# One fused attention and expert kernel on one core: other first steps, a plain product for the row of maxima, and new orders of the pairs

## The chip, the cores and the metric

The kernel runs on one core of a Trainium2 chip. The metric is the device time of one execution in microseconds (us); the program is built for that core alone and uses no other. Engines are named as the profile names them: PE (TensorE, matrix products; PEld are its weight loads), DVE (VectorE), ACT (ScalarE), POOL (GpSimd) and SP (SyncE, which here only issues DMAs).

## The reference

All inputs are float32. Attention with pooled queries comes first, then a soft mixture of experts, then a gated network:

```python
q_pool = q.reshape(B, H, S // 2, 2, D).mean(axis=3)            # B, H, S, D = 4, 8, 1152, 64
scores = q_pool @ k.transpose(0, 1, 3, 2) / np.sqrt(D)
attn = np.exp(scores - scores.max(-1, keepdims=True))
attn = attn / (attn.sum(-1, keepdims=True) + 1e-9)
x = (attn @ v).transpose(0, 2, 1, 3).reshape(2304, 512)
logits = x @ phi                                               # 8 experts x 4 slots
d = softmax of logits over the tokens; slot_input = d.T @ x
slot_out[e] = relu(slot_input[e] @ w1[e]) @ w2[e]
x = softmax of logits over the slots @ slot_out
xn = x / sqrt(mean(x * x) + 1e-6) * rms_g
out = (silu(xn @ w_gate) * (xn @ w_val)) @ w_out
```

The change touches attention alone, the first 430 us or so.

## The kernel before, in words

**Pairs.** The 32 heads of attention are worked on two at a time, in 16 pairs; one head of a pair lies in partitions 0 to 63, the other in 64 to 127. A pair has 576 pooled queries, cut in two halves `h` of 288, and 1152 keys, cut in nine tiles `kt` of 128.

- `qk` (a step `q31` is tile 3, half 1; lines 374 to 388): a score tile, the keys in partitions and 288 queries of each head in columns, in a double bank of PSUM. Four products of each head are added up: high keys by high queries, low keys by high queries, high keys by low queries (keys and queries are split into a rounded part and a rest), and `pick` by `mr`, which subtracts each query's maximum. ACT then writes `e`, the exponential.
- `add_e` (a step `e31`): POOL adds up `e` over the tiles, for the sums. The first of each group adds nothing.
- `av` (a step `v31`, or `v3` for both halves; lines 403 to 412): the products of `e` and the values, in plain float32, four products side by side, each with 32 columns of weights.
- `max_item` (a step `m`; lines 289 to 335): products of queries and keys whose maximum DVE reads straight from PSUM. Pair 0 has 14 of them, of 384 columns; the eight with numbers 0 to 7 run before the first score, and 0 to 2 and 3 to 5 are the queries' first two tiles with the three chunks of keys, 6 and 7 the products with `tb`, the last 64 queries of both heads in one block. The later pairs have eleven of up to 512 columns, of which `ta` and `tb` stand in the pair before.
- The nine maxima of a query tile set are reduced once more (`max_red`), turned into a row by TensorE (`max_row`, lines 342 to 347), negated by ACT into `mrow`, and copied into `mr` by four DMAs (`send_row`). In pair 0 a first part goes another way, without DMA: `first_max` turns the maxima by products with an identity, and DVE spreads the result over `mr` in one scaling (lines 359 to 371). `row_0` is `max_row` and `send_row` of pair 0's rest.

**Side steps.** While a pair p runs, its list of steps also prepares later pairs and finishes earlier ones: `load_q`, `load_k`, `sum_q`, `round_k`, `high_q`, `block_q` (which fills `tb`), `less_k` for p + 2; `rest_k`, `low_q`, `load_v`, `max_red`, `max_row`, `send_row` for p + 1; `take_x`, `sums`, `inverse`, `x_logits`, `x_turn`, `recips`, `logit_add`, `x_divide` for p - 1 (the sums are inverted, the outputs turned and divided). Every fourth pair adds a softmax over tokens (`d_turn`, `d_exp`, `d_back`, `d_copy`, `slot_part`, `slot_copy`, `slot_turn`) or over slots (`c_turn`, `c_exp`, `c_soft`). Weights of the last network come as 64-bit data by `load_64`, are converted by ACT (`abs_64`, two instructions) and DVE (`turn_64`), and are written back to memory by `spill`.

**Order.** The order is written out by hand in lists: `FIRST` for pair 0, `PLAN` for pairs 1 to 13, `LAST_2` for pair 14, `LAST` for pair 15. Each engine and each queue of DMAs (SP's, and POOL's for `rest_k` and `sum_q`) works on its own steps in the order of the list, and waits only for data or for room. PSUM's eight banks are four double banks in attention: one holds `av` from its first product to `take_x`, and score tiles, maxima and all small results share the rest. Steps that find no room in SBUF for a weight leave their load to a later step.

**The start.** Lines 790 to 837 stand ahead of the lists. SP loads pair 0's queries and keys in chunks; ACT rounds three chunks of keys, `kc`; DVE and POOL add up the queries; `block_q(0)` fills `tb`; then come the eight first maxima and `first_max`. `hold` (lines 198 to 201) issues products that nothing reads; the kernel uses it only behind attention.

Of the kernel before, what the change touches and what calls it, by code (L numbers as in the profile page):

```python
# [31 lines left out]
NMAX = 9  # L32
AHEAD = 0
FIRST = """
m m round_k1 round_k1 less_1 m rest_1 q00 q10 m e10 m m q70 m q20 q30 e30 q50 q40 load_q m row_0 q60 m e50 block_q1
q80 e20 v50 m e60 m m v30 e70 v20 e40 v60 v10 sum_q q61 q01 low_q q21 q31 q51 e31 e00 q41 m e41 q81 q11 e01 q71 m e81
m v40 e11 e71 m m max_red v70 v01 e51 e21 v00 high_q load_k block_q e61 round_k round_k e80 v80 v31 max_row load_v tb
less_k ta v21 v41 v51 send_row v11 v71 v61 v81
"""
PLAN = """  # L40
take_x load_q m load_k sum_q q00 q01 q10 m q11 q20 e00 q21 m e01 e10 e20 e11 c_exp q30 e30 q31 rest_k q40 load_ew e21
c_soft m e31 q41 e40 q50 e41 m e50 q51 q60 q61 q70 turn_64 m load_ew spill e60 q71 q80 q81 round_k round_k m m m e70
e51 load_v e80 sums v0 v1 abs_64 e61 abs_64 e71 v2 d_back load_64 e81 max_red v3 v4 x_logits less_k inverse d_copy
inverse high_q block_q c_soft max_row low_q x_turn recips abs_64 logit_add slot_part c_soft pair_up x_divide x_divide
turn_64 v5 v6 d_turn send_row tb c_turn ta slot_copy turn_64 d_exp drop_x slot_turn c_soft v7 load_64 load_64 v8
"""
LAST_2 = """
take_x load_q m load_k sum_q q00 q01 load q10 m q11 load q20 e00 load q21 m e01 e10 e20 e11 c_exp load q30 e30 q31
rest_k load q40 load_ew e21 c_soft m e31 load q41 e40 load q50 e41 m e50 q51 load q60 load q61 q70 turn_64 m load_ew
spill e60 q71 load q80 q81 round_k round_k m m m e70 e51 load_v e80 sums v0 v1 abs_64 e61 abs_64 e71 v2 d_back load_64  # L50
e81 max_red v3 v4 x_logits less_k inverse d_copy inverse high_q block_q c_soft max_row low_q x_turn recips abs_64
logit_add slot_part c_soft pair_up x_divide x_divide turn_64 v5 v6 d_turn send_row tb c_turn ta slot_copy turn_64
d_exp drop_x slot_turn c_soft v7 load_64 load_64 v8
"""
LAST = """
take_x q00 load_64 sum_up sum_up load_q load_k load q01 e00 e01 c_exp turn_64 load_ew load q10 load q11 spill e10 e11
# [39 lines left out]
def attention_softmoe_gated_kernel(ctx: ExitStack, tc: tile.TileContext, kT, qT, vv, ip, cst, w1, w2, wg, wv, wo, rg, out):  # L96
    nc = tc.nc
    dv, ac, pe, gp, sy = nc.vector, nc.scalar, nc.tensor, nc.gpsimd, nc.sync
# [18 lines left out]
    def A(shape, dt, name):  # L117
        return take("A", shape, dt, name)
# [53 lines left out]
    def S(shape, name, dt=F32, bufs=2, tag=None):  # L172
        return small.tile(shape, dt, tag=tag or name, name=name, bufs=bufs)

    def two_banks(name):
        return ps.tile([128, 2, 512], F32, tag="u", bufs=4, name=name)
# [27 lines left out]
    ident, stack = cs[:, 0:128], cs[:, 128:256]  # L204
# [9 lines left out]
    mxw = one.tile([128, 128], F32, name="mxw")  # L214
    sall = one.tile([32, 5], F32, name="sall")
    mr = [one.tile([128, 576], F32R, name=f"mr{i}") for i in range(2)]
    pick = [one.tile([128, 128], F32R, name=f"pick{i}") for i in range(2)]
    tb = one.tile([128, 128], F32R, name="tb")
# [41 lines left out]
    def block_q(p):  # L260

        for s in range(2):
            r = slice(64 * s, 64 * s + 64)
            ac.copy(tb[r, r], qh[p][r, 512:576] if p else qh[p][r, 256:320])
# [24 lines left out]
    def max_item(p, i):  # L289

        if p not in mx3:
            mx3[p] = S([128, 2 * NQT + 1, 3], "mx3")
        if p:
            return wide_item(p, i)
        o = two_banks("mxp")
        if i not in (6, 7):
            t, c = divmod(i - 2 if i > 7 else i, 3)
            at = 128 * t if t < 2 else 128 * t + 64
            for s in range(2):
                r = slice(64 * s, 64 * s + 64)  # L300
                pe.matmul(o[:, s, 0:KC], lhsT=qh[p][r, at:at + 128], rhs=kh[p][r, KC * c:KC * c + KC], start=True, stop=True)
            to = mx3[p][:, 0:2 * NQT].rearrange("p (s t) c -> p s t c", s=2)[:, :, t, c]
            dv.reduce_max(out=to, in_=o[:, :, 0:KC], axis=AX.X)
        else:
            n = 8 - i
            for j in range(n):
                c = 2 * (i - 6) + j
                pe.matmul(o[:, j, 0:KC], lhsT=tb, rhs=kh[p][:, KC * c:KC * c + KC], start=True, stop=True)
            dv.reduce_max(out=mx3[p][:, 2 * NQT, 2 * (i - 6):2 * (i - 6) + n], in_=o[:, 0:n, 0:KC], axis=AX.X)

    def wide_item(p, i):

        o = two_banks("mxp")
        q, k, m = qh[p], kh[p], mx3[p]
        heads = m[:, 0:2 * NQT].rearrange("p (s t) c -> p s t c", s=2)
        rest = slice(1024, 1152)
        if i < 8:
            c, t = divmod(i, 4)
            for s in range(2):
                r = slice(64 * s, 64 * s + 64)  # L320
                pe.matmul(o[:, s, :], lhsT=q[r, 128 * t:128 * t + 128], rhs=k[r, 512 * c:512 * c + 512], start=True, stop=True)  # L321
            dv.reduce_max(out=heads[:, :, t, c], in_=o, axis=AX.X)  # L322
        elif i == 8:
            for t in range(NQT):
                for s in range(2):
                    r = slice(64 * s, 64 * s + 64)
                    pe.matmul(o[:, s, 128 * t:128 * t + 128], lhsT=q[r, 128 * t:128 * t + 128], rhs=k[r, rest], start=True, stop=True)  # L327
            dv.reduce_max(out=heads[:, :, :, 2], in_=o.rearrange("p s (t k) -> p s t k", t=NQT), axis=AX.X)
        elif i == 9:
            for c in range(2):  # L330
                pe.matmul(o[:, c, :], lhsT=tb, rhs=k[:, 512 * c:512 * c + 512], start=True, stop=True)  # L331
            dv.reduce_max(out=m[:, 2 * NQT, 0:2], in_=o, axis=AX.X)
        else:
            pe.matmul(o[:, 0, 0:128], lhsT=tb, rhs=k[:, rest], start=True, stop=True)
            dv.reduce_max(out=m[:, 2 * NQT, 2:3], in_=o[:, 0:1, 0:128], axis=AX.X)
# [6 lines left out]
    def max_row(p):  # L342
        n = 2 * NQT + 1
        o = bank([128, 128], "mxt")
        pe.transpose(out=o[0:32], in_=mxw[:, 0:32], identity=ident)
        rows[p] = S([n, 128], "mrow", F32R, bufs=1)
        ac.mul(rows[p], o[0:n], -1.0)

# [7 lines left out]
            sy.dma_start(out=f(to[:, 0:512]).rearrange("p (t i) -> p t i", i=128), in_=f(row[NQT * s:NQT * s + NQT, :]))  # L356
            sy.dma_start(out=f(to[:, 512:576]), in_=f(row[2 * NQT:2 * NQT + 1, 64 * s:64 * s + 64]))

    def first_max():

        dv.reduce_max(out=mxa[0:64, 2:3], in_=mx3[0][0:64, 2 * NQT, 0:3], axis=AX.X)
        dv.reduce_max(out=mxb[64:128, 66:67], in_=mx3[0][64:128, 2 * NQT, 0:3], axis=AX.X)
        dv.reduce_max(out=mxa.rearrange("p (s c) -> p s c", s=2)[:, :, 0:2],
                      in_=mx3[0][:, 0:2 * NQT].rearrange("p (s t) c -> p s t c", s=2)[:, :, 0:2], axis=AX.X)
        o = bank([128, 128], "mxt")
        r = slice(0, 67)
        pe.matmul(o[r], lhsT=mxa[:, r], rhs=ident, start=True, stop=False)
        pe.matmul(o[r, 0:64], lhsT=mxb, rhs=ident[:, 64:128], start=False, stop=True)
        dv.scalar_tensor_tensor(out=mr[0][r, 0:384].rearrange("p (t i) -> p t i", t=3),
                                in0=o[r, None, :].to_broadcast([67, 3, 128]), scalar=-1.0,  # L370
                                in1=stack[r, 0:3, None].to_broadcast([67, 3, 128]), op0=ALU.mult, op1=ALU.mult)
# [249 lines left out]
    n = HELD_O  # L621
# [167 lines left out]
    with tc.manual_schedule():  # L789
        q0 = qraw[0] = A([128, 2, 576], F32, "qraw")  # L790
        k0 = kraw[0] = A([128, 1152], F32, "kraw")
        mxa = mxw
        mxb = S([128, 67], "mxb", bufs=1, tag="ct")
        qa, qb = slice(0, 384), slice(384, 576)
        kc = [slice(KC * c, KC * c + KC) for c in range(3)]
# [6 lines left out]
        kh0 = kh[0] = A([128, 1152], F32R, "kh")  # L802
# [10 lines left out]
        qs0 = qs[0] = B([128, 576], F32, "qs")  # L813
        qh0 = qh[0] = B([128, 576], F32R, "qh")
        dv.tensor_tensor(out=qh0[:, qa], in0=q0[:, 0, qa], in1=q0[:, 1, qa], op=ALU.add)
        for c in kc:
            ac.copy(kh0[:, c], k0[:, c])
        gp.tensor_tensor(out=qs0[:, qa], in0=q0[:, 0, qa], in1=q0[:, 1, qa], op=ALU.add)
        low_k(0, kc[0], gp)
        gp.tensor_tensor(out=qs0[:, qb], in0=q0[:, 0, qb], in1=q0[:, 1, qb], op=ALU.add)  # L820
        rel("A")
        ac.copy(qh0[:, qb], qs0[:, qb])
        block_q(0)
        low_q(0, gp)
        low_k(0, kc[1], gp)
        low_k(0, kc[2], gp)
# [1 line left out]
        high_q(1)  # L828
        load_v(0)
        load_k(1)  # L830
        for i in (0, 1, 2, 6, 7, 3, 4, 5):
            max_item(0, i)
        first_max()
        dv.memset(half, -0.5)
        sy.dma_start(out=ipt, in_=ip.rearrange("p (a b) -> p a b", a=4))
# [46 lines left out]
        o = accum("xl")  # L882
# [6 lines left out]
        r = rr[l]  # L889
        o = accum("by")  # L890
# [20 lines left out]
        for i in range(3):  # L911
            for s in range(2):
                c = slice(64 * s, 64 * s + 64)
# [33 lines left out]
        o = bank([128, 3, 32], "br")  # L947
# [10 lines left out]
        o = bank([128, 4, 32], "pto")  # L958
# [156 lines left out]
        o = bank([128, 4, 32], "gto")  # L1115
# [6 lines left out]
        o = bank([128, 32], "gram")  # L1122
# [118 lines left out]
        for step in SEQ:  # L1241
            n = int(step[1:] or 0)
# [29 lines left out]
        for g in range(1, NG):  # L1272
            for t in range(3):
                for c in [slice(0, 512)] if (g, t) != (NG - 1, 2) else [slice(128 * i, 128 * i + 128 * n) for i, n in TAIL]:
                    o = ps.tile([128, c.stop - c.start], F32, tag="av", bufs=2, name="yo")
# [42 lines left out]
```

## Time and profile before

| | |
|---|---|
| median of 3 runs | 680.61 us (680.22 to 681.07) |
| profiled execution | 682.14 us, its span 680.4 us |
| PE busy | 663.7 us, 98% of the span |
| DVE, ACT, POOL busy | 432.7, 403.6, 457.4 us |
| HBM traffic | 99.29 MB read, 14.16 MB written |

The span runs from the first to the last instruction of the profiled execution. A line of a timeline gives the start, the duration of all that it merges, the engine, the line of the kernel, the operation, what it writes and reads with the shapes, how many instructions (x2), and in brackets the idle time of the engine before it and what ended that. Matrix products are pipelined: each one's duration includes the time until its result is out, so that the pace is read from the starts. A line of the chain of waits gives the start, the share of time and the work that the end hung on just then.

### The profile page before, as it was taken

How to read it: one execution, taken by the hardware profiler on the slowest of the kernel's cores; microseconds unless marked ns; L12 is line 12 of the kernel's file. 1: busy time of each engine (PE TensorE's matmuls, PEld its weight loads, DVE VectorE, ACT ScalarE, POOL GpSimd, SP SyncE). 2: the span in 40 equal slices, each digit the busy share in tenths (PEclk: the TensorE clock that was granted, in tenths of full speed). 3: DMA queues.
4: the chain of work that ended last, by engine and by line, in shares of the span. 5: the costliest groups of instructions: out<-in, count | busy, mean ns of one | idle time of the engine just before them, and what ended most of it. 6: DMA issues, size and time to landing. Idle time of an engine off the chain costs nothing.

```text
span 680.4 us, 17782 instructions
## 1 busy us (share of the span) xinstructions
PE 663.7 (98%) x7319; PEld 487.2 (72%) x7319; DVE 432.7 (64%) x595; ACT 403.6 (59%) x814; POOL 457.4 (67%) x368
## 2 busy tenths in 40 slices
PE   3999999999999999999999999999899999999998
PEld 2776876866876866867767766543577788888887
DVE  5867678877888887888887766420546755444410
ACT  4566867967768868768867625331456645444420
POOL 6689789989969989789899675000357754534420
PEclk9999999999999999999999999999999999999999
DMA  6333855976966965666675659899940100000000
GB/s 224 105 121 60 242 153 157 289 233 150 265 224 183 302 189 131 185 213 164 191 204 135 228 158 341 304 347 390 385 183 1 47 32 32 15 32 32 31 32 31
DMA packets 57784, 114.66 MB, mean 169 GB/s; under 512 B 6252, under 2 KB 20072, under 8 KB 57704
## 3 DMA queue, kind: packets, MB, share of 16 engines
q1 hardware_dynamic: 53672, 100.86, 43.2%
q0 software_dynamic: 4032, 12.68, 10.7%
q8 instruction: 57, 0.93, 0.5%
q14 instruction: 23, 0.19, 0.1%
HBM read 99.29 MB, written 14.16 MB: 167 GB/s over the span
## 4 chain that ended last, share of the span: by engine, by line
PE 87%; DVE 4%; DMA 4%; issue 1%; ACT 1%; POOL 1%; DVEq 0%; POOLq 0%; ACTq 0%; SPq 0%
PE sc L383 22%; PE av L408 21%; PE yo L1219 19%; PE mxp L321 5%; PE gv L1171 3%; DMA w<-away 3%; PE sums L431 3%; PE hin L980 2%; PE xo L471 1%; DMA w<-in_w_dram 1%; PE so L1005 1%; PE mxp L331 1%; PE xl L489 1%; PE mxp L327 1%; PE pp L551 1%
## 5 line engine op out<-in xcount | busy, mean ns | idle before, releaser
L401 POOL TENSOR_TENSOR acc<-acc,e 128x576 f32<-128x576 f32 x153 | 233.3, 1541 | 9.9 <-ACT e L385 3.5
L385 ACT ACTIVATE e<-sc 128x576 f32<-128x576 f32 x288 | 168.6, 652 | 29.8 <-PE sc L383 25.9
L322 DVE TENSOR_REDUCE mx<-mxp 128x2 f32<-128x1024 f32 x120 | 145.5, 1224 | 51.2 <-PE mxp L321 49.9
L408 PE MATMUL av<-e,vt 128*32 128x288 f32 x2304 | 151.0, 408 | 0.0
L408 PEld LDWEIGHTS av<-e,vt 128*32 128x32 f32 x2304 | 74.2, 110 | 61.1 <-issue 7.8
L401 POOL TENSOR_TENSOR acc<-e 128x576 f32<-128x576 f32 x63 | 100.8, 1601 | 17.1 <-ACT e L385 17.0
L1219 PE MATMUL yo<-woh,hA 128*128 128x512 f32 (+1 forms) x312 | 98.8, 385 | 0.2 <-POOL hA L1202 0.2
L383 PE MATMUL sc<-qh,kh 64*128 64x288 f32 x576 | 88.8, 303 | 0.4
L383 PE MATMUL sc<-qh,kl 64*128 64x288 f32 x576 | 86.1, 294 | 0.0
L383 PE MATMUL sc<-mr,pick 64*128 64x288 f32 x576 | 86.0, 293 | 0.0
L383 PE MATMUL sc<-ql,kh 64*128 64x288 f32 x576 | 85.9, 293 | 0.0
L1202 POOL TENSOR_TENSOR hA<-hu,hA 128x384 fp32r<-128x384 f32 x48 | 48.7, 1017 | 44.0 <-ACT hA L1201 43.9
L1176 DVE SCALAR_TENSOR_TENSOR th<-th,gv 128x384 f32<-128x384 f32 x72 | 39.8, 553 | 55.8 <-ACT th L1173 55.6
L1219 PEld LDWEIGHTS yo<-woh,hA 128*128 128x128 f32 x312 | 57.6, 188 | 10.8 <-POOL hA L1202 1.1
L1173 ACT ACTIVATE th<-gv 128x384 f32<-128x384 f32 x72 | 35.1, 490 | 50.1 <-PE gv L1171 47.7
L383 PEld LDWEIGHTS sc<-qh,kh 64*128 64x128 f32 x576 | 55.1, 187 | 8.5 <-DVE mx L322 5.8
L1219 PE MATMUL yo<-wol,hA 128*128 128x512 f32 (+1 forms) x151 | 57.9, 383 | 0.0
L383 PEld LDWEIGHTS sc<-qh,kl 64*128 64x128 f32 x576 | 55.3, 187 | 3.0
L383 PEld LDWEIGHTS sc<-ql,kh 64*128 64x128 f32 x576 | 55.2, 187 | 0.0
L383 PEld LDWEIGHTS sc<-mr,pick 64*128 64x128 f32 x576 | 55.1, 186 | 0.0
L321 PE MATMUL mxp<-kh,qh 64*128 64x512 f32 x240 | 48.0, 417 | 0.3
L698 DVE SCALAR_TENSOR_TENSOR w<-w,raw 128x512 uint32<-128x512 uint32 x36 | 44.9, 1248 | 0.3 <-ACT raw L696 0.3
(211 smaller groups left out, 1025.6 us busy)
## 6 DMA issues: line engine op xcount, KB each, us to landing
w<-in_w_dram SPq DMA_DIRECT2D x84, 256.0 KB
w<-in_w_dram SPq DMA_DIRECT2D x22, 512.0 KB
vt<-in_vv_dram SPq DMA_DIRECT2D x16, 576.0 KB
away<-w SPq DMA_DIRECT2D x36, 256.0 KB
w<-away SPq DMA_DIRECT2D x36, 256.0 KB
kraw<-in_kT_dram SPq DMA_DIRECT2D x15, 576.0 KB
kl<-in_kT_dram POOLq DMA_DIRECT2D x15, 576.0 KB, 7.4
raw<-in_wg_dram SPq DMA_DIRECT2D x12, 512.0 KB
```

The costliest lines, as they stand in the source:

```text
L321: pe.matmul(o[:, s, :], lhsT=q[r, 128 * t:128 * t + 128], rhs=k[r, 512 * c:512 * c + 512], start=True, stop=True)
L322: dv.reduce_max(out=heads[:, :, t, c], in_=o, axis=AX.X)
L383: pe.matmul(o[:, s, 0:HQ], lhsT=w[r, wk], rhs=q[r, c], start=(i == 0), stop=(i == 3))
L385: ac.activation(ets[p, kt, h], o[:, :, 0:HQ], AF.Exp, scale=0.0625)
L401: eng.tensor_tensor(out=acc[p, h, j], in0=first[p, h, j] if n == 1 else acc[p, h, j], in1=e, op=ALU.add)
L408: pe.matmul(avt[p][g:g + 32, h, 0:HQ], lhsT=vt[p][:, kt, g:g + 32], rhs=ets[p, kt, h][:, g // 64], start=(n == 1), stop=(n == NKT))
L431: pe.matmul(o[g:g + 32, :], lhsT=ones, rhs=acc[p, h, j][:, s], start=(j == 0), stop=(j == n - 1))
L698: dv.scalar_tensor_tensor(out=y, in0=y, scalar=3, in1=lo, op0=ALU.logical_shift_left, op1=ALU.bitwise_or),
L1173: ac.activation(t, o[0], AF.Tanh, scale=0.5)
L1176: dv.scalar_tensor_tensor(out=t, in0=t, scalar=1.0, in1=o[0], op0=ALU.add, op1=ALU.mult)
L1202: gp.tensor_tensor(out=b, in0=u, in1=f(a), op=ALU.subtract)
L1219: pe.matmul(o, lhsT=x, rhs=w[:, c], start=(ft == 0 and i == 0), stop=(ft == NF - 1 and i == 2))
```

## The change

**Start.** `block_q(0)` moves from behind the last piece of the queries to ScalarE's first copy of keys. The eight first maxima are taken in another order. Ahead of them stand six, and behind each of them two, pairs of products of 288 columns into a double bank `warm` that nothing reads; their operands are zeros and a one-hot block that POOL has filled by then. The two small reductions of the `tb` maxima move ahead of the last two items, and the three products of `first_max` become three groups of 64 columns, the one with `mxb` first.

**Row of maxima.** `max_row` no longer uses the transposing mode; it multiplies by the identity, in float32.

**Orders.** `FIRST`, `PLAN` and `LAST_2` are new (`LAST_2` is `PLAN` with eleven `load` steps put in, as before). `LAST` stays.

```diff
 FIRST = """
-m m round_k1 round_k1 less_1 m rest_1 q00 q10 m e10 m m q70 m q20 q30 e30 q50 q40 load_q m row_0 q60 m e50 block_q1
-q80 e20 v50 m e60 m m v30 e70 v20 e40 v60 v10 sum_q q61 q01 low_q q21 q31 q51 e31 e00 q41 m e41 q81 q11 e01 q71 m e81
-m v40 e11 e71 m m max_red v70 v01 e51 e21 v00 high_q load_k block_q e61 round_k round_k e80 v80 v31 max_row load_v tb
-less_k ta v21 v41 v51 send_row v11 v71 v61 v81
+m m round_k1 q30 q20 m m round_k1 less_1 q50 rest_1 m m q40 q10 q70 load_q e10 m row_0 q80 m e20 e50 q00 q60 m m e40 m
+v50 sum_q v20 e30 v10 low_q v40 q61 e00 e70 q21 q31 q01 m q41 q71 e61 q11 q51 e71 m v30 e60 e01 m high_q load_k q81
+e31 m e41 e11 v60 block_q1 v11 m m e81 block_q max_red e80 e21 v01 v71 v80 v81 e51 round_k round_k max_row v41 v70 ta
+load_v tb send_row v00 v31 v61 v51 less_k v21
 """
 PLAN = """
-take_x load_q m load_k sum_q q00 q01 q10 m q11 q20 e00 q21 m e01 e10 e20 e11 c_exp q30 e30 q31 rest_k q40 load_ew e21
-c_soft m e31 q41 e40 q50 e41 m e50 q51 q60 q61 q70 turn_64 m load_ew spill e60 q71 q80 q81 round_k round_k m m m e70
-e51 load_v e80 sums v0 v1 abs_64 e61 abs_64 e71 v2 d_back load_64 e81 max_red v3 v4 x_logits less_k inverse d_copy
-inverse high_q block_q c_soft max_row low_q x_turn recips abs_64 logit_add slot_part c_soft pair_up x_divide x_divide
-turn_64 v5 v6 d_turn send_row tb c_turn ta slot_copy turn_64 d_exp drop_x slot_turn c_soft v7 load_64 load_64 v8
+take_x m load_q q00 load_k e00 q01 q10 e01 m q11 q20 sum_q q21 e10 e11 c_exp m e20 q30 c_soft e21 e30 q31 rest_k q40 m
+e31 q41 e40 load_ew q50 load_v e50 m q51 e41 q60 e60 q61 load_ew turn_64 q70 m spill q71 q80 q81 m round_k round_k
+abs_64 m e51 e61 e70 m max_red sums v0 v1 abs_64 less_k v2 e71 load_64 v3 v4 d_back x_logits inverse high_q e81
+inverse e80 d_copy c_soft low_q slot_part max_row x_turn recips block_q abs_64 logit_add pair_up load_64 x_divide
+x_divide c_soft c_soft load_64 turn_64 v5 v6 tb ta d_turn c_turn slot_copy slot_turn v7 turn_64 v8 send_row drop_x
+d_exp
 """
...
     def max_row(p):
         n = 2 * NQT + 1
         o = bank([128, 128], "mxt")
-        pe.transpose(out=o[0:32], in_=mxw[:, 0:32], identity=ident)
+        pe.matmul(o[0:32], lhsT=mxw[:, 0:32], rhs=ident, start=True, stop=True)
...
-    def first_max():
+    def first_tail():
 
         dv.reduce_max(out=mxa[0:64, 2:3], in_=mx3[0][0:64, 2 * NQT, 0:3], axis=AX.X)
         dv.reduce_max(out=mxb[64:128, 66:67], in_=mx3[0][64:128, 2 * NQT, 0:3], axis=AX.X)
+
+    def first_max():
+
...
-        r = slice(0, 67)
-        pe.matmul(o[r], lhsT=mxa[:, r], rhs=ident, start=True, stop=False)
-        pe.matmul(o[r, 0:64], lhsT=mxb, rhs=ident[:, 64:128], start=False, stop=True)
+        r, c0, c1 = slice(0, 67), slice(0, 64), slice(64, 128)
+        pe.matmul(o[r, c0], lhsT=mxb, rhs=ident[:, c1], start=True, stop=False)
+        pe.matmul(o[r, c0], lhsT=mxa[:, r], rhs=ident[:, c0], start=False, stop=True)
+        pe.matmul(o[r, c1], lhsT=mxa[:, r], rhs=ident[:, c1], start=True, stop=True)
...
-        for c in kc:
+        ac.copy(kh0[:, kc[0]], k0[:, kc[0]])
+        block_q(0)
+        for c in kc[1:]:
             ac.copy(kh0[:, c], k0[:, c])
...
         ac.copy(qh0[:, qb], qs0[:, qb])
-        block_q(0)
...
-        for i in (0, 1, 2, 6, 7, 3, 4, 5):
+        warm = two_banks("hold")
+
+        def unread(n):
+            for _ in range(n):
+                for s in range(2):
+                    r = slice(64 * s, 64 * s + 64)
+                    pe.matmul(warm[:, s, 0:288], lhsT=pick[0][r], rhs=mr[1][r, 0:288], start=True, stop=True)
+
+        unread(6)
+        for i in (0, 3, 1, 4, 6, 7, 2, 5):
             max_item(0, i)
+            unread(2)
+            if i == 7:
+                first_tail()
         first_max()
```

## Rows read from the trace of the kernel before

**Rows 1.** The page: busy time by engine; the chain that ended last, by engine.
```profile
PE 663.7 (98%) x7319; PEld 487.2 (72%) x7319; DVE 432.7 (64%) x595; ACT 403.6 (59%) x814; POOL 457.4 (67%) x368
...
PE 87%; DVE 4%; DMA 4%; issue 1%; ACT 1%; POOL 1%; DVEq 0%; POOLq 0%; ACTq 0%; SPq 0%
```

**Rows 2.** Timeline of the start: start us, duration us, engine, line, operation.
```profile
6.14 0.51 ACT L817 CAST kh<-kraw 128x384 fp32r<-128x384 f32 x1 [0.48 <-DMA kraw<-in_kT_dram]
...
6.45 1.95 DVE L303 TENSOR_REDUCE mx<-mxp 128x2 f32<-128x768 f32 x2 [1.26 <-PE mxp L301]
...
8.76 0.49 ACT L264 CAST tb<-qh 64x64 fp32r<-64x64 f32 x2
...
10.41 1.42 DVE L309 TENSOR_REDUCE mx<-mxp 128x2 f32<-128x768 f32 x2 [0.87 <-PE mxp L308]
...
11.75 2.68 DVE L303 TENSOR_REDUCE mx<-mxp 128x2 f32<-128x768 f32 x3
...
14.34 0.13 DVE L361 TENSOR_REDUCE mxw<-mx 64x1 f32<-64x3 f32 x1
...
15.16 0.67 PE L367 MATMUL mxt<-cs,mxw 128*67 128x128 f32 x2 [3.05 <-DVE mxw L363]
...
15.51 1.25 ACT L284 ACTIVATE kl<-kh 128x576 fp32r<-128x576 f32 x2
15.61 0.43 PE L368 MATMUL mxt<-cs,mxb 128*67 128x64 f32 x2
...
16.08 0.55 DVE L369 SCALAR_TENSOR_TENSOR mr<-mxt,cs 67x384 fp32r<-67x384 f32 x1 [1.22 <-PE mxt L368]
```

**Rows 3.** Chain of waits from 14.5 to 30 us: start us, us, what.
```profile
14.70 0.18 DVE mxw L363
...
25.88 0.62 PE av L408 x8
```

**Rows 4.** Timeline around the first scores.
```profile
17.09 0.44 PE L383 MATMUL sc<-qh,kh 64*128 64x288 f32 x2
...
17.33 0.44 PE L383 MATMUL sc<-qh,kl 64*128 64x288 f32 x2
...
18.30 0.65 ACT L385 ACTIVATE e<-sc 128x576 f32<-128x576 f32 x1 [1.54 <-PE sc L383]
...
21.70 0.29 PE L383 MATMUL sc<-qh,kl 64*128 64x288 f32 x2
...
21.83 0.29 PE L383 MATMUL sc<-ql,kh 64*128 64x288 f32 x2
...
22.30 0.18 DVE L340 TENSOR_REDUCE mxw<-mx 128x9 f32<-128x27 f32 x1
```

**Rows 5.** Windows: stretch, its length, busy us by engine, then clock, DMA share, GB/s.
```profile
18.00:20.00 2.00, 2.00 (x20) 1.67 (x16) 1.81 (x3) 1.30 (x2) 0.14 (x1) 1.00 0.66 74
```

**Rows 6.** Timelines of DVE and of PE near 101 us, in pair 3.
```profile
100.10 1.23 DVE L322 TENSOR_REDUCE mx<-mxp 128x2 f32<-128x1024 f32 x1 [0.60 <-PE mxp L321]
...
101.38 0.40 PE L383 MATMUL sc<-qh,kh 64*128 64x288 f32 x2
```

**Rows 7.** Chain of waits from 81 to 106 us, the second half of a middle pair.
```profile
87.52 0.48 PE xl L489 x8
88.00 0.21 PE mxt L345
88.22 0.66 PE xo L471 x6
...
89.20 2.08 PE av L408 x32
```

**Rows 8.** Line 345: duration ns min/median/max, first and last start us, shape.
```profile
L345 PE MATMUL mxt<-cs,mxw x16: 284/285/287, 24.1 to 399.3; 128*32 128x128 f32 x16
```

**Rows 9.** Chain of waits from 189 to 200 us: `c_turn` in pair 6.
```profile
194.77 0.51 PE lgt L583 x6
```

**Rows 10.** Waits of SP from 60 to 400 us: us in total, times, longest.
```profile
SPq L356 <- ACT mrow L347: 135.2, 14, 18.6
```

More of the change, by code (lines that the diff above doesn't have):

```diff
@@ L46 @@
+abs_64 m e51 e61 e70 m max_red sums v0 v1 abs_64 less_k v2 e71 load_64 v3 v4 d_back x_logits inverse high_q e81
+inverse e80 d_copy c_soft low_q slot_part max_row x_turn recips block_q abs_64 logit_add pair_up load_64 x_divide
+x_divide c_soft c_soft load_64 turn_64 v5 v6 tb ta d_turn c_turn slot_copy slot_turn v7 turn_64 v8 send_row drop_x
+d_exp
 """
 LAST_2 = """
-take_x load_q m load_k sum_q q00 q01 load q10 m q11 load q20 e00 load q21 m e01 e10 e20 e11 c_exp load q30 e30 q31
-rest_k load q40 load_ew e21 c_soft m e31 load q41 e40 load q50 e41 m e50 q51 load q60 load q61 q70 turn_64 m load_ew
@@ L50 @@
[L50 to L53, printed above, removed]
+take_x m load_q q00 load_k e00 q01 load q10 e01 m q11 load q20 sum_q load q21 e10 e11 c_exp m e20 load q30 c_soft e21
@@ new lines @@
+e30 q31 rest_k load q40 m e31 load q41 e40 load_ew load q50 load_v e50 m q51 e41 load q60 e60 load q61 load_ew turn_64
+q70 m spill q71 load q80 q81 m round_k round_k abs_64 m e51 e61 e70 m max_red sums v0 v1 abs_64 less_k v2 e71 load_64
+v3 v4 d_back x_logits inverse high_q e81 inverse e80 d_copy c_soft low_q slot_part max_row x_turn recips block_q
+abs_64 logit_add pair_up load_64 x_divide x_divide c_soft c_soft load_64 turn_64 v5 v6 tb ta d_turn c_turn slot_copy
+slot_turn v7 turn_64 v8 send_row drop_x d_exp
```

## The prediction

> **What bounds the kernel now.** I read the page first: TensorE is busy 98% of 680.4 us and holds 87% of the chain that ended last [rows 1]. Little is left over, so an edit counts only where TensorE idles, is slow, or gets more to do. The chain of waits and the timeline, read in order of time, then show three kinds of stretch.
>
> At the start the chain is not TensorE's. The reader should follow VectorE: its eight first maxima run from 6.45 to 14.43 us, with a hole of 0.87 us ahead of 10.41, where the products with `tb` wait for ScalarE's copies of 8.76; then come three small maxima, ended at 14.88, 0.28 us of issue, four matrix products and one scaling, ended at 16.63, which the first score needs [rows 2, 3].
>
> From 17 us on the same score product appears at half pace: a step every 0.24 us for 288 columns, 1.2 GHz, against 0.13 us at 21.7 us, 2.4 GHz [rows 4]. The windows' clock column says 1.00 there too [rows 5], so the pace must be read from the steps. TensorE had idled for 3.05 us before 15.16 [rows 2]; from there it worked almost without a pause until the pace rose.
>
> In the middle pairs TensorE follows itself. Two small exceptions come back: a score product waits for a bank whose maximum VectorE reads until 101.33 (it starts at 101.38, some 0.3 us late) [rows 6], and about 0.1 us goes where TensorE turns from products with 32 columns of weights (`av`, `xl`) to another shape [rows 7].
>
> **The change part by part.** All sums are against the profiled execution (span 680.40, time 682.14 us, so 1.74 us lie around the span); the median of the runs is 680.61 us, 1.53 us under it, and I carry that difference over unchanged.
>
> *First maxima.* The new order puts two maxima of the first chunk of keys first, then two of the second, then the `tb` ones, and `block_q(0)` moves ahead of ScalarE's second copy. That copy waits 0.48 us for its DMA, and the two `tb` copies take 0.49 [rows 2], so they fit in that hole. VectorE then has none: 6.45 + four at 0.97 + 1.42 (the two `tb` ones) + 0.36 (two small ones, now ahead of the last two) + 2 x 0.89 + 0.18 = 14.07 us, against 14.88. Gain 0.8 us. TensorE must feed it: even at 1.2 GHz a maximum's product (384 columns, 0.32 us) and two unread pairs (2 x 0.24) take 0.8 us, under 0.97. The unread tile holds one of four double banks; with three left, each product still finds one that was read a reduction earlier. The cover for the unread products is this wait for VectorE; where it is gone, a group of two costs its own 0.48 us.
>
> *Turning the first maxima.* Six products of 64 columns replace two of 128 and two of 64, and the two with `mxb` can go ahead of the last maximum. Behind it that leaves 256 columns instead of 384 in steps of 0.22 us per 128 at 1.2 GHz [rows 2]: 0.2 us off, at 2.4 GHz some 0.4. The scaling ends at 15.4 to 15.6 us instead of 16.63.
>
> *First pair.* A schedule by hand at 2.4 GHz, with 0.90 us for a reduction [rows 2], 0.53 (four steps) for a score product, 0.65 for its exponential [rows 4], 0.18 to 0.23 for a maximum's product (384 and 512 columns at that pace), and four double banks, each free once VectorE or ScalarE has read it. VectorE makes six reductions from 15.5 on: 16.4, 17.3, 18.2, 19.1, 20.0, 20.9, and the last one over them (0.18) ends at 21.1 instead of 22.48 [rows 4]. TensorE stands in line behind them, in the order `m m q30 q20 m m q50 m m q40 q10 q70 m`: q30 done at 15.6, q20 16.1, third maximum from 16.4, fourth 17.05, q50 from 17.3, fifth maximum 18.2, sixth 19.1, q40 19.5 (its bank is q50's, whose exponential stands behind `less_1`'s 1.25 us on ScalarE [rows 2]), q10 to 20.6, q70 20.8 to 21.4, seventh maximum to 21.8. Then `row_0` (0.45, below), q80, q00, q60 and four maxima, with some 0.2 for banks, bring the first `av` product to 24.95 us. In the trace it starts at 25.88 [rows 3], with the same nine score products done, but two maxima fewer (0.46): a lead of 0.93 + 0.46 = 1.4 us. The rest of the pair has the same work and one turn between shapes more; I take 0.2 us off for that and the second row: **1.2 us** gained. Bounds: if the old pace lasts to 20.6 us, three scores cost 0.43 more each, of which VectorE's line covers little, and 0.2 is left; with hardly a bank wait it would be 2.4.
>
> *Row of maxima.* Sixteen rows are turned [rows 8], fourteen of them in pairs 1 to 14. Now each is one transposed pass; in the chain it holds 0.21 us, of which 0.11 is the pass (six transposes of 128 columns take 0.66) and the rest the turn from `xl`'s shape [rows 7]. A plain float32 product shows two instructions, as the four of the first maxima do [rows 2]. At 2.4 GHz the plain `av` products take 2.08 us for 32, four side by side, so 0.26 a pass of 288 columns [rows 7] and 0.116 for 128; two passes 0.23. The turn between shapes stays, only behind the row instead of ahead of it. Extra: 0.11 us a pair, with nothing to hide it, since TensorE does not pause there: 14 x 0.11 = **1.5 us** lost. Bounds: 0 (a pass hidden in the turn) and 0.45 - 0.11 = 0.34 each (both passes at the first maxima's step of 0.22). In pair 0 `row_0` stands among products of the wide shape and gets two turns of 0.11 besides, counted above.
>
> *Rest of the middle order.* I wrote out TensorE's steps of old and new order side by side. Up to the last maximum they are identical, so the bank wait stays, and `turn_64` keeps its place on VectorE. Behind it `d_back`, `slot_part`, `d_turn` and `c_turn` move, with the same count of turns between shapes: `c_turn` between the two `tb` products held 0.51 us [rows 9] and takes as long behind them. ScalarE's order changes (a conversion goes ahead of the sums' copy, `block_q` behind the reciprocals), but I found no result wanted before it comes; nearest are `d_back`'s copy ahead of `slot_part` and `slot_copy` ahead of `slot_turn`, three pairs each. On POOL `sum_q` still precedes the pair's first addition. I take zero; not below, as TensorE has no pause there to win back; above, one instruction of an exponential's length late in each of three pairs, 2.0 us.
>
> *SP's queue.* `send_row`'s four DMAs now stand behind three weight loads, and `load_v` ahead of the write-out that waits for VectorE. SP waited 135.2 us for the row in fourteen pairs [rows 10], so loads issued ahead fit into that wait, provided that their slots are free: by my count they were last read by the scores and copies of the same pair, before the `av` products. I take zero; if not, see the fourth rival.
>
> Sum: -1.2 + 1.5 = +0.3 us: 682.14 becomes 682.4, the median 680.61 becomes **680.9 us**. The later stages start with attention's end and move along.
>
> **Rule and row.** In the trace a transposed pass of 128 columns takes 0.11 us, a plain pass 0.116, and there are two: a factor of two [rows 7]. The Trainium skill ("TensorE: Matmul & The Clock Gate", Terms) calls transposing four times faster for float32; by that each row would cost 0.33 us more and the kernel end near the third rival's time; the rows speak against it.
>
> **Rivals.**
> 1. *The row costs nothing* (0.20). Its second pass hides in the turn to the transposes and the start gives 1.2 to 2.4 us: 678.2 to 679.4, centre 678.8. For it: where shapes agree, weight loads hide. Against: in [rows 7] the passes stand in file, with no pause to fill.
> 2. *The clock does not hold* (0.14). VectorE's pace leaves TensorE partly idle from 6 to 21 us, and it works at 1.2 GHz up to the scores as now. Gain 0.2, loss 1.5: 681.9. For it: the slow stretch followed a thin one. Against: at that pace the unread products keep it busy for 0.8 of every 0.97 us.
> 3. *Slower: a costly second pass* (0.07). Place: between `xl` and the transposes of every pair. 14 x 0.34 - 1.2 = +3.6: 684.2. It decides from 0.18 us a row on ((1.36 + 1.2) / 14); at 0.086 the change is neutral. For it: the first maxima's steps. Against: those ran at 1.2 GHz.
> 4. *The row arrives late* (0.05). If a load ahead of `send_row` waits for a raw weight that `turn_64` has not read, the next pair's first score waits for `mr`: one VectorE step of 0.9 us in thirteen pairs, +12: 693.
>
> **How the numbers follow.** My forecast has 0.54. A measurement tells 0.2%, 1.36 us, from no change: faster is under 679.25, slower over 681.97. Faster: 0.17 of the first rival and 0.05 of the forecast, 0.22. Slower: 0.07, 0.05, 0.06 of the second and 0.02 of the forecast, 0.20. Same: 0.58. The range leaves out the far half of the first rival and most of the third and fourth: 678.7 to 682.6.
>
> **What would show it.** First maxima ended near 14.07 us; score steps of 0.13 us from the first on; the first `av` near 25.0 and the first `xu` copy 1.2 us earlier; two matmuls a row, from `xl` to `xo` 0.11 us longer, pairs 1 to 14 each 0.1 us longer. Wrong if the pairs differ by more than 0.3 us either way, if steps of 0.24 us remain after 17 us, or if a score product waits for `mr`.

## The result, and the profile after

The changed kernel is slower: a median of 688.58 us (688.14 to 690.4, five runs) against 680.62 us of the kernel before beside it, ratio 1.011 with a 95% interval of 1.0095 to 1.0126. The forecast was 680.9 us, its range ended at 682.6, and no rival named what happened. The profiled execution has a span of 687.2 us, 6.8 more than before.

The page first; the rows answer to [rows 1]:

```profile
PE 668.9 (97%) x7381; PEld 489.5 (71%) x7381; DVE 459.5 (67%) x595; ACT 401.0 (58%) x814; POOL 448.6 (65%) x368
...
PE 75%; DVE 12%; issue 5%; DMA 5%; ACT 1%; POOL 1%; SPq 0%; DVEq 0%; ACTq 0%; POOLq 0%
```

VectorE has as many instructions as before, 595, and is busy 26.8 us longer. It holds 12% of the chain instead of 4, and "issue", time in which nothing that the profile shows is waited for, 5% instead of 1. An engine that does the same work in more time is either working at another pace or being kept out; which, the durations by line tell.

**Where attention's time went.** The `xu` copies (one a pair, line 416 before and 421 after) cut attention into its pairs. The first starts at 42.80 us (44.22 before), the last at 433.91 (427.39): the start gives 1.42 us, the fifteen pairs take 391.11 us instead of 383.17, 7.94 more, and behind them some 0.3 are added. That is the 6.8 us. Pairs 1 and 2 grow by 0.1 us each, as the row should make them; pairs 3 to 13 by 0.4 to 1.3, past the 0.3 us at which the prediction called itself wrong.

**The start** came out as forecast in its sum. Timeline, to be read beside [rows 2, 4], and below it a line of the chain beside [rows 3]:

```profile
14.47 0.17 DVE L367 TENSOR_REDUCE mxw<-mx 128x4 f32<-128x12 f32 x1
...
15.18 0.55 DVE L374 SCALAR_TENSOR_TENSOR mr<-mxt,cs 67x384 fp32r<-67x384 f32 x1 [0.55 <-PE mxt L373]
...
15.53 0.30 PE L388 MATMUL sc<-qh,kh 64*128 64x288 f32 x2
15.66 0.30 PE L388 MATMUL sc<-qh,kl 64*128 64x288 f32 x2
```

```profile
24.84 1.33 PE av L413 x17
```

The scaling ends at 15.73, the score steps are 0.13 us apart from the first on, and the first `av` is 1.04 us earlier.

**The row** too. Chain of waits of a middle pair, beside [rows 7]:

```profile
86.14 0.48 PE xl L494 x8
86.62 0.22 PE mxt L346 x2
86.84 0.79 PE xo L476 x6
```

The row's products hold what they held; the turn of `xu` behind them grew from 0.66 to 0.79 us. Extra 0.13 to 0.14 a pair, forecast 0.11.

**What nobody looked at: `low_q`.** This is VectorE's subtraction `ql = qs - qh`, 128 x 576, unchanged by the diff. Its line before, then after (count, ns min/median/max, first and last start):

```profile
L268 DVE TENSOR_TENSOR ql<-qs,qh x15: 741/1057/1718, 30.4 to 397.8; 128x576 fp32r<-128x576 f32 x15
```

```profile
L269 DVE TENSOR_TENSOR ql<-qs,qh x15: 1766/3730/4291, 27.5 to 404.1; 128x576 fp32r<-128x576 f32 x15
```

The same instruction on the same shape takes 3.5 times as long; the fifteen together grow by 39 us (`turn_64`'s 36 shrink by 10, from 44.9 to 34.9 us). Beside it run POOL's additions. Timelines of POOL and of VectorE in the same pair (p = 2), before:

```profile
79.92 0.87 POOL L287 DMA_DIRECT2D kl<-in_kT_dram  x1
80.53 1.71 POOL L401 TENSOR_TENSOR acc<-acc,e 128x576 f32<-128x576 f32 x1
...
82.32 4.19 POOL L401 TENSOR_TENSOR acc<-acc,e 128x576 f32<-128x576 f32 x3
86.47 1.92 POOL L401 TENSOR_TENSOR acc<-e 128x576 f32<-128x576 f32 x1
...
86.35 0.77 DVE L268 TENSOR_TENSOR ql<-qs,qh 128x576 fp32r<-128x576 f32 x1
88.09 0.47 DVE L497 TENSOR_TENSOR xl<-xl,srow 128x288 f32<-128x288 f32 x1 [0.97 <-PE xl L489]
```

and after:

```profile
77.64 0.83 POOL L288 DMA_DIRECT2D kl<-in_kT_dram  x1
78.25 4.44 POOL L406 TENSOR_TENSOR acc<-acc,e 128x576 f32<-128x576 f32 x3
82.40 1.67 POOL L406 TENSOR_TENSOR acc<-e 128x576 f32<-128x576 f32 x1
83.79 3.02 POOL L406 TENSOR_TENSOR acc<-acc,e 128x576 f32<-128x576 f32 x2
86.53 1.63 POOL L406 TENSOR_TENSOR acc<-e 128x576 f32<-128x576 f32 x1
88.24 4.21 POOL L406 TENSOR_TENSOR acc<-acc,e 128x576 f32<-128x576 f32 x2
...
85.06 3.73 DVE L269 TENSOR_TENSOR ql<-qs,qh 128x576 fp32r<-128x576 f32 x1
88.71 0.45 DVE L502 TENSOR_TENSOR xl<-xl,srow 128x288 f32<-128x288 f32 x1
```

Read the ends against the next starts. Before, POOL issued `rest_k` (line 287), ran one addition of 1.71 us, and paused (82.24 to 82.32); the three from there take 4.19 us, and each next one starts as the last ends. `low_q` got in at the first boundary, at 86.47, and the addition there became 1.92 us long. After, from `rest_k` on, each addition starts 0.3 us before the one ahead of it is recorded as ended (83.79, 85.16 and 86.53, 1.63 to 1.67 us each), for seven in a row. `low_q` starts at 85.06, sees two ends of additions pass, and ends 0.6 us behind 88.16, where POOL pauses for 0.08 us. So its duration is a wait for a pause of POOL, and 0.6 us of its own work.

What decides on a pause is the order of the additions. POOL keeps four running sums (two halves of the queries, two groups of tiles each). An addition that needs the sum of the one just ahead of it has to wait for it: that is the pause. The old `PLAN` has such neighbours between `rest_k` and `low_q`, `e21 e31` and `e60 e70`. The new one has `e31 e40 e41 e60 e51 e70 e71 e81`: halves and groups alternate, and only `e81` follows its own sum.

The length costs time only where VectorE has no room for it. The pair shown, p = 2, grew by 0.1 us although its `low_q` took 3.73 us, and so did pair 1 with 3.86 (pair 14 grew by 0.2 with 3.66). In the kernel before, VectorE was busy 17.6, 19.3 and 17.7 us of the 25 in pairs 1, 2 and 14, against 20.0 to 22.0 us in pairs 3 to 13, where TensorE now comes to wait for it.

Before, VectorE waited 0.97 us for `xl` behind `low_q` (the bracket at 88.09); after, it does not wait but is late. Waits of TensorE from 30 to 430 us, none of which stands in the list before, and the chain of a pair with `slot_part`:

```profile
PE xo L476 <- DVE lg L506: 3.0, 3, 1.0
...
PE mxp L335 <- DVE lg L503: 0.9, 3, 0.3
```

```profile
162.33 0.06 DVE ql L269
162.38 4.07 issue
166.46 0.46 DVE lg L506
...
166.96 0.86 PE xo L476 x6
```

The chain has no name for being kept out: it calls the 4.07 us "issue". Seven such pieces, of 2.95 to 4.07 us, are most of the page's 5%.

The Trainium skill ("SBUF — State Buffer", Who interferes with whom) says that a VectorE instruction with two inputs in SBUF contends with a GpSimd instruction that reads SBUF, and (Summary: rules for kernel authors) that of the two the second one to issue is blocked until the first has finished. The trace agrees on who contends (`low_q` is of that kind). On how long it differs: `low_q` is kept out until POOL pauses, past two ends of additions here, and past five in a pair of experiment 6.

### The profile page after: what moved, and what is told of

Its sections match the earlier page's. It is cut to its first block, busy times and chain, and to the rows that moved or that the text cites. A ratio compares the mean times of both kernels' runs of the same rounds, so it can differ in the third digit from the quotient of the medians.

```text
span 687.2 us, 17941 instructions
## 1 busy us (share of the span) xinstructions
PE 668.9 (97%) x7381; PEld 489.5 (71%) x7381; DVE 459.5 (67%) x595; ACT 401.0 (58%) x814; POOL 448.6 (65%) x368
## 4 chain that ended last, share of the span: by engine, by line
PE 75%; DVE 12%; issue 5%; DMA 5%; ACT 1%; POOL 1%; SPq 0%; DVEq 0%; ACTq 0%; POOLq 0%
PE sc L388 22%; PE yo L1237 20%; PE av L413 13%; PE mxp L322 4%; DVE mx L323 3%; PE gv L1189 3%; DMA w<-away 3%; PE hin L998 2%; DVE w L703 1%; DVE srow L460 1%; PE sums L436 1%; DMA w<-in_w_dram 1%; PE xo L476 1%; DVE mx L329 1%; PE so L1023 1%
## 5 line engine op out<-in xcount | busy, mean ns | idle before, releaser
L406 POOL TENSOR_TENSOR acc<-acc,e 128x576 f32<-128x576 f32 x153 | 236.9, 1651 | 6.4 <-ACT e L390 3.4
L390 ACT ACTIVATE e<-sc 128x576 f32<-128x576 f32 x288 | 168.8, 651 | 29.9 <-PE sc L388 26.5
L406 POOL TENSOR_TENSOR acc<-e 128x576 f32<-128x576 f32 x63 | 97.1, 1551 | 41.1 <-ACT e L390 39.5
L269 DVE TENSOR_TENSOR ql<-qs,qh 128x576 fp32r<-128x576 f32 x15 | 55.0, 3665 | 0.0
```

The lines of the kernel that those rows point to most:

```text
L269: eng.tensor_tensor(out=ql[p], in0=qs[p], in1=f(qh[p]), op=ALU.subtract)
L390: ac.activation(ets[p, kt, h], o[:, :, 0:HQ], AF.Exp, scale=0.0625)
L406: eng.tensor_tensor(out=acc[p, h, j], in0=first[p, h, j] if n == 1 else acc[p, h, j], in1=e, op=ALU.add)
```

## The experiments

Times stand beside the kernel before on the same chip (681.0 to 681.1 us). "Pairs" is the first to the last `xu` copy of the profile: 383.17 us before, 391.11 after.

**1. The old orders of the middle pairs in the changed kernel.** `PLAN` and `LAST_2` as before, all else as changed.

> The changed kernel with the old PLAN and LAST_2; new start, new FIRST and plain row stay. Theory (the new order of the middle pairs locks VectorE's low_q out behind POOL's additions): low_q falls from a mean of 3.67 us to about 1.0, the start's 1.4 us gain and the rows' loss of 14 x 0.13 = 1.8 us are left, 680.6 - 1.4 + 1.8 = 681.0 us. Rival (the plain row, or the new start and FIRST, cost the 8 us): 688 us.

680.95 us, ratio 0.9995 (0.9983 to 1.0007); `low_q` 1.19 us in the mean, pairs 383.91. The loss goes with the new orders, and neither the row nor the start carries it.

**2. The row turned as before, in the changed kernel.**

```diff
-        pe.matmul(o[0:32], lhsT=mxw[:, 0:32], rhs=ident, start=True, stop=True)
+        pe.transpose(out=o[0:32], in_=mxw[:, 0:32], identity=ident)
```

> The changed kernel with the transposing mode back in max_row, all else as changed. Theory (lockout): only the rows' 14 x 0.13 us come back, 686.7 us, low_q stays at 3.7 us. Rival (the second pass of the plain row is the loss, directly or through what it delays): 680 to 681 us.

687.85 us, ratio 1.0095 (1.0078 to 1.0113), pairs 389.83, `low_q` 3.57 us. The rival falls. Only 1.3 us come back, not 1.8. Pairs 3, 4, 6, 8, 10 and 12 give back 0.02 us at most, pair 5 alone 0.63. It fits that in a pair that waits for VectorE anyway the row's second pass lies in the wait; why pair 5 gives so much is open.

**3. `rest_k` behind `low_q`.** One step moved in `PLAN` and `LAST_2`.

> The changed kernel with one step moved: rest_k, a DMA that POOL issues, stands directly behind low_q in PLAN and LAST_2. Theory (POOL's additions overlap one another from rest_k's issue until POOL next pauses, and low_q gets in only at a pause): no overlapped additions stand ahead of low_q any more, it takes 0.8 to 1.7 us as in the kernel before, and most of 6 us comes back: 682 to 684 us. Rival 1 (the new order of ScalarE's and TensorE's steps costs the time, low_q is only late with it): 688 us, low_q short or not. Rival 2 (the additions overlap because they stand ready, whatever rest_k does): low_q stays at 3 to 4.3 us and the time at 688 us.

`low_q` did as the theory says: it gets in at the next end of an addition, in most pairs with no pause there. The time did not: 773.08 us, ratio 1.136 (1.132 to 1.140), a price that I had not seen. Durations of `low_q`; waits; issues of DMAs (KB each, median us to landing):

```profile
L268 DVE TENSOR_TENSOR ql<-qs,qh x15: 695/1472/1770, 27.4 to 478.5; 128x576 fp32r<-128x576 f32 x15
```

```profile
PE sc L387 <- DMA kl<-in_kT_dram: 65.0, 12, 7.9
```

```profile
kl<-in_kT_dram POOLq DMA_DIRECT2D x15, 576.0 KB, 8.0
```

`rest_k` takes 8.0 us to land, and stands behind POOL's additions in POOL's queue; moved behind nine more of them it is late for the next pair's second score product. Besides these waits the granted clock reads 0.50 (1.2 GHz) for 78.5 us in all, each time from within or just behind such a wait on. The run tells that the overlapping comes with `rest_k`'s issue; on the price of `low_q` it tells nothing.

**4. `rest_k` two additions later, in the kernel before** (just ahead of `e40`).

> The kernel before with one step moved: rest_k goes two of POOL's additions further, to just ahead of e40, in PLAN and LAST_2. Theory: from rest_k's issue POOL runs e40, e41 and e60 in overlapped form, low_q falls among them and takes 3 to 4 us instead of 1.04; the time rises by 3 to 6 us, to 683.6 to 686.6. Rival (low_q's length comes with the other new steps and not with rest_k): low_q near 1 us, time 680.6 us.

```profile
L268 DVE TENSOR_TENSOR ql<-qs,qh x15: 719/1782/3103, 29.8 to 397.3; 128x576 fp32r<-128x576 f32 x15
```

681.44 us, ratio 1.001 (0.9997 to 1.0023): no loss to be told from none. The dose was too small: POOL still paused ahead of `e70`, `low_q` grew by 0.8 us in the mean, and the old order has about 1 us behind it in which VectorE waits for `xl` (88.09 above). It fits that its price starts only past that.

**5. `e70` ahead of `e51`, in the changed kernel.** The smallest step that gives POOL a pause back:

```diff
-abs_64 m e51 e61 e70 m max_red sums
+abs_64 m e70 e51 e61 m max_red sums
```

> The changed kernel with one step moved: e70 stands ahead of e51 in PLAN and LAST_2, so that on POOL it follows e60, which writes the same accumulator. Theory (an addition that needs the sum of the one just ahead of it has to wait for it, POOL pauses some 0.08 us, and this ends both the overlapping and VectorE's wait; the old order had such neighbours, e21 e31 and e60 e70, between rest_k and low_q, the new one has none): a pause appears near 16.4 us of each pair, low_q falls from 3.67 to between 0.7 and 1.8 us, and some 6 us come back: 681.5 to 683.5 us. Rival 1 (other steps of the new order cost the time): low_q short, time 687 to 688.6 us. Rival 2 (the overlap depends on rest_k alone): low_q stays near 3.7 us, time 688.6 us.

```profile
L269 DVE TENSOR_TENSOR ql<-qs,qh x15: 720/1666/1801, 28.8 to 397.2; 128x576 fp32r<-128x576 f32 x15
```

Timelines of POOL and VectorE in the same pair as above, and the chain of the pair with `slot_part`:

```profile
82.25 1.64 POOL L406 TENSOR_TENSOR acc<-acc,e 128x576 f32<-128x576 f32 x1
83.64 1.64 POOL L406 TENSOR_TENSOR acc<-e 128x576 f32<-128x576 f32 x1
...
85.36 3.30 POOL L406 TENSOR_TENSOR acc<-acc,e 128x576 f32<-128x576 f32 x2
...
86.24 1.15 DVE L269 TENSOR_TENSOR ql<-qs,qh 128x576 fp32r<-128x576 f32 x1
87.89 0.47 DVE L502 TENSOR_TENSOR xl<-xl,srow 128x288 f32<-128x288 f32 x1 [0.50 <-PE xl L494]
```

```profile
165.62 0.20 PE mxt L346 x2
165.82 0.79 PE xo L476 x6
```

The pause is there (85.28 to 85.36), `low_q` is short, VectorE waits for `xl` again, and the "issue" piece has left the chain. 679.71 us, ratio 0.9982 (0.9971 to 0.9992): 8.9 us between the medians of the two (8.7 by their ratios to the kernel before), from one addition moved ahead of one other, more than the 6 expected; pairs 382.96. From the start's rise to the end of attention the granted clock reads 1.00 in both profiles. Both rivals fall.

**6. The reverse, in the kernel before:** `e31` behind `e40` and `e41` behind `e60`, so that no pause is left between `rest_k` and `e81`.

> The kernel before with two additions moved, e31 behind e40 and e41 behind e60, so that between rest_k and low_q no addition needs the sum of the one ahead of it; nothing else changes. Theory: POOL's additions overlap from rest_k to e81, low_q takes 3 to 4.3 us in most pairs instead of 1.04, and the time rises by 3 to 6 us to 684 to 687 us. Rival 1 (the pause has nothing to do with the accumulators): low_q about 1 us, time 681 us. Rival 2 (low_q long but with room behind it in the old order): low_q over 3 us, time under 682.5 us.

```profile
L268 DVE TENSOR_TENSOR ql<-qs,qh x15: 1132/5253/7790, 29.9 to 428.3; 128x576 fp32r<-128x576 f32 x15
```

```profile
113.36 5.77 POOL L401 TENSOR_TENSOR acc<-acc,e 128x576 f32<-128x576 f32 x4
118.86 1.64 POOL L401 TENSOR_TENSOR acc<-e 128x576 f32<-128x576 f32 x1
120.58 1.81 POOL L401 TENSOR_TENSOR acc<-acc,e 128x576 f32<-128x576 f32 x1
...
115.64 5.49 DVE L268 TENSOR_TENSOR ql<-qs,qh 128x576 fp32r<-128x576 f32 x1
```

714.21 us, ratio 1.0485 (1.0464 to 1.0505). The direction is the theory's, the size I expected was five to eleven times too small: POOL's list runs later in the old order, so `e81`'s pause comes only 4.9 us behind `low_q`'s start. With 4.2 us more a `low_q` the time rises by 33 us, some 2.2 us a pair; with 0.8 more (experiment 4) by nothing. Not all of it is waiting: of the 32.3 us by which the pairs grew, TensorE's fourteen waits for VectorE (1.2 to 3.8 us each) hold 24.2. The rest fits a lower pace of TensorE. Window in pair 4; stretch, its length, busy us by engine, then clock, DMA share, GB/s:

```profile
150.40:157.10 6.70, 6.17 (x39) 2.28 (x39) 4.85 (x10) 0.82 (x2) 1.74 (x2) 0.50 0.82 258
```

The granted clock reads 0.50, 1.2 GHz, in four stretches of 17.1 us together, in pairs 1, 4, 5 and 9, each within or just behind one of TensorE's long waits (1.75, 3.79, 2.35 and 2.24 us). At half the pace that is up to 8.5 us of the rise.

**7. The start alone:** the kernel before with the new start and `FIRST`.

> The kernel before with the new start and the new FIRST alone; old PLAN and LAST_2, and the row turned in the transposing mode as before. Theory: the start's 1.2 to 1.4 us are all that is left, 679.2 to 679.6 us against 680.6 to 681.0 us; beside the kernel with old orders and plain row, some 1.8 us less. Rival (the earlier start is lost again in the first pairs, by transfers that come no earlier): 680.6 us or more.

681.06 us, ratio 0.9999 (0.9985 to 1.0013): in the median the gain is not there. The profiled execution (681.92 us) shows why in its own score steps:

```profile
16.02 0.44 PE L387 MATMUL sc<-qh,kh 64*128 64x288 f32 x2
16.26 0.44 PE L387 MATMUL sc<-qh,kl 64*128 64x288 f32 x2
...
18.44 0.30 PE L387 MATMUL sc<-qh,kh 64*128 64x288 f32 x2
18.57 0.30 PE L387 MATMUL sc<-qh,kl 64*128 64x288 f32 x2
```

Steps of 0.24 us up to 18 us: 1.2 GHz. Of the eight profiles of the new start (that of the result and those of 1, 2, 3, 5, 7, 8, 9), six have 0.13 us from the first score on and the first `xu` copy at 42.0 to 42.8 us; two (5 and 7) have 0.24 us and it starts at 44.0 to 44.1. Before it started at 43.6 to 44.2 in three profiles. So the second rival of the prediction is true in some executions. The twelve times of experiment 5 agree: eight lie from 679.4 to 680.1 us, four from 681.0 to 681.3, and the profiled one, at the low pace, is one of the four.

**8 and 9. The best of both:** experiment 5 with the row in the transposing mode, and the same kernel again, later on the same chip.

> The same kernel with the transposing mode back in max_row: new start, new orders with e70 ahead of e51. If the terms add up, 14 x 0.13 = 1.8 us less than with the plain row: 679.7 to 681.7 us, and near 679.5 us if the new order of the middle pairs is then worth exactly the old one. Rival (the row's price was measured beside a stall that hid or doubled it): the difference from the kernel with the plain row lies under 0.8 or over 2.6 us.

> The kernel with new start, new orders, e70 ahead of e51 and the row turned in the transposing mode once more, beside the next two on one chip. As before, 678.0 us. Of the profiles of the new start so far four show score steps of 0.13 us from the first score on and two show 0.24 us up to 18.4 us, with the first xu copy at 42.0 to 42.8 and at 44.0 to 44.1 us; which of the two this one shows is open.

678.03 us, ratio 0.9951 (0.9933 to 0.9968), and 679.29 us, ratio 0.9986 (0.9962 to 1.001; one of its twelve runs took 687.48): two medians of one kernel, 1.3 us apart. Pairs 381.52 and 381.08, against 382.96 with the plain row: 1.4 to 1.9 us, the terms add up. Against experiment 7, which has the old orders and the same row (383.34), the new orders with their pause are worth 1.8 to 2.3 us.

**10 and 11. Twelve unread pairs instead of six ahead of the first maximum, and none at all,** in the kernel of 8.

> The same with twelve pairs of unread products instead of six ahead of the first maximum, so that TensorE does not idle from 4.2 to 5.5 us, when the first keys have come. Theory (the clock rises late in part of the executions because TensorE pauses there): score steps of 0.13 us from the first on, first xu copy at 42.0 to 42.8 us, median at least 0.4 us under the kernel with six. Rival 1 (it is the later, thin stretches from 9 to 11 us that decide): both paces still occur, median as with six. Rival 2 (the unread products hold the first maximum up): first maximum later than 6.7 us, slower than with six.

> The same without any unread product. Theory (they raise the pace, where it rises): score steps of 0.24 us past 17 us in the profile, first xu copy near 44 us, time 0.5 to 1.4 us over the kernel with them. Rival (the new order of maxima and scores alone makes the start shorter): first xu copy at 42 to 43 us, time equal.

Twelve: 678.39 us, ratio 0.9965 (0.995 to 0.9979). The pace rose earlier and was lost again; timeline of TensorE:

```profile
7.11 0.43 PE L843 MATMUL hold<-mr,pick 64*128 64x288 f32 x4
...
12.26 0.30 PE L371 MATMUL mxt<-cs,mxb 128*67 128x64 f32 x2 [0.25 <-PE hold L843]
14.27 0.49 PE L372 MATMUL mxt<-cs,mxw 128*67 128x64 f32 x2 [1.71 <-DVE mxw L367]
...
15.72 0.44 PE L388 MATMUL sc<-qh,kh 64*128 64x288 f32 x2
15.96 0.44 PE L388 MATMUL sc<-qh,kl 64*128 64x288 f32 x2
```

Four unread products take 0.43 us at 7.11 us, 2.4 GHz, and the scores are back at 0.24 a step, against the theory. The window shows the granted clock at 0.50:

```profile
13.60:20.40 6.80, 6.13 (x42) 5.50 (x44) 5.22 (x10) 4.11 (x8) 0.00 (x0) 0.50 0.07 25
```

From 6.8 to 13.5 us it reads 1.00. At the higher pace TensorE finishes each group early and pauses for VectorE, 1.71 us ahead of 14.27, and the clock falls in that pause; but in the profile of the result it pauses 1.55 us there and the clock stays at 1.00. The mean granted clock is 0.995 to 0.997 in ten of the twelve executions, and the two at 0.999 and 1.0 are the shortest, 677.24 and 677.4 us. So the filled pause at 4.2 us brings the pace earlier and doesn't make it last, and what does is open. None: 678.8 us, ratio 0.9965 (0.9951 to 0.9978), steps of 0.24 us, first `xu` copy at 43.44 us: without them the new order of the first maxima alone gives 0.2 to 0.8 us against the three profiles of the old start. What the unread products are worth in the median can't be told from nothing here; in an execution where the pace holds they give another 0.6 to 1.4 us.

## Why the prediction was wrong, step by step

- **What failed is the term "Rest of the middle order": "I take zero; not below, as TensorE has no pause there to win back; above, one instruction of an exponential's length late in each of three pairs, 2.0 us."** I checked for each moved step whether a result is wanted before it comes, and on POOL only that "`sum_q` still precedes the pair's first addition". The durations of unmoved instructions I carried over from the trace of before. But the moved additions changed the duration of one: `low_q` went from 1.04 to 3.67 us in the mean, VectorE was late for `logit_add` and the maxima, and TensorE waited. With row and start equal, the orders cost 389.83 - 383.34 = 6.5 us of pairs (experiments 2 and 7), 4.5 us past the upper bound. The reason for the lower one does not hold either: with the pause back, the orders give 1.8 to 2.3 us. That the order of POOL's additions makes the difference, experiments 5 and 6 show from both sides.
- **It could be read in the trace of before:** a subtraction of one shape that takes 741 to 1718 ns waits for something, and it always ended some 0.6 us behind a boundary of POOL's. None of the rows that I chose showed VectorE's and POOL's instructions beside each other.
- **First pair, -1.2 us:** near for the profiled execution (-1.42), in part because misses cancel. First maxima ended at 14.64 instead of 14.07 (the first one began 0.23 us later, the rest is gaps between 10.2 and 12.3 us in which VectorE waited for TensorE at 1.2 GHz). The turning then took 0.24 to 0.44 us less than forecast, and the stretch from the scaling to the first `av` as much less again. And it holds only where the clock rises, in six profiles of eight. I gave that rival 0.14.
- **Row of maxima, +1.5 us:** 0.13 to 0.14 a pair; in all 1.4 to 1.9 us with the pause back, 1.3 in the changed kernel, 0.6 between experiments 1 and 7 (why so little there, is open). The factor of two between the passes held: two a row, 0.11 us apart.
- **SP's queue, 0:** right. SP waits 82.6 us for the row instead of [rows 10], and no score waits for `mr`.

## What to carry to other kernels

In this kernel VectorE's subtraction and POOL's additions both read SBUF, and the order of the additions set how long the subtraction took. In another, compare the durations of VectorE's two-input instructions for one shape, and lay them beside POOL's timeline before moving either. Neighbours that need each other's result look like something to schedule away; here that small pause of 0.08 us was what let the other engine in, and taking it out of the kernel before cost 2.2 us a pair in the mean, a quarter of it at most by TensorE's lower clock behind its waits. "Issue" on a chain, at an instruction with a long and varying duration, is a wait without a name.

## What the runs showed that I had not expected

- From the issue of a DMA on POOL on, its additions are recorded as 1.6 to 1.7 us long and overlap by about 0.3 us; a pause of 0.08 us ends this, and then they stand end to end (1.42 us each). In both kinds the starts are 1.38 us apart. VectorE's subtraction gets in at any end of the second kind (0.7 to 1.9 us), and only at a pause in the first (up to 7.79 us). In the thirteen profiles 192 of the 195 subtractions end some 0.6 us behind a boundary, 64 of these pauses and 128 ends of the second kind; all 96 boundaries that they let pass are overlaps. Why the two kinds differ, no run here shows.
- TensorE's pace at the start differs between executions of the same start, with the first `xu` copy at 42.0 or at 44.1 us. The windows read 1.00 in both, but ahead of the rise that is no reading, in [rows 5] neither: the trace has no record of the clock before 9.0 to 11.0 us in the six profiles, 18.3 and 18.5 us in the two, and 20.75 us in the kernel before, and these are the times at which the steps shorten.
- What in the new orders, once the pause is back, gives 1.8 to 2.3 us against the old ones was not separated. A candidate is `turn_64`, which also ends behind POOL's boundaries: before, 26 of its 36 instructions took 0.9 to 1.9 us and the others 0.7; after, 10 took 1.4 to 1.9. Its sum falls from 44.9 over 34.9 to 29.9 us in experiment 5.
